# Query tails by transfer, logits summed over heads on GpSimd, guard add on VectorE

## The chip, the cores and the metric

The kernel runs on one core of one Trainium2 chip. The metric is device time in microseconds (us) for one execution, lower is better. Its engines are named by the profile: PE is TensorE (matrix products; PEld its weight loads), DVE is VectorE, ACT is ScalarE, POOL is GpSimd, SP is the engine whose queue issues most DMAs. Each engine takes its instructions strictly in the order in which the program emits them.

## The reference, cut to what matters

```python
# attention: B=4 batches, H=8 heads, S=576 rows, D=64
scores = q @ k.T / 8                       # per batch and head
thresh = scores.max(-1) - tau
scores = where(scores >= thresh, scores, -1e9)
attn = exp(scores - scores.max(-1))
attn = attn / (attn.sum(-1) + 1e-9)        # 1e-9 is the "guard"
x = (attn @ v) laid out as (2304 tokens, 512)

# mixture of 8 experts, two chosen per token
logits = x @ w_gate
noisy = logits + log1p(exp(x @ w_noise)) * noise
top2 = the two largest of the 8; top2_w = softmax of the two (+ 1e-9 in the sum)
x = sum over both of top2_w * (relu(x @ w1[e]) @ w2[e])

# a last two-layer network
h = x @ w_in
out = (max(h, 0) + alpha * min(h, 0)) @ w_out
```

## The kernel before

The first quarter of the kernel, up to about 300 us, is attention with the gating woven into it; after it come the experts and the last network, which are matrix products throughout. The change touches the first quarter alone.

**Units.** Attention is cut into 80 units. A unit is a batch, a pair of heads, and 128 query rows; since 576 is four times 128 plus 64, each batch has a rest of 64 rows, and a "t" unit (16 of the 80) handles the rest of both heads of a pair at once. Units 0 to 15 run over the rows for each head pair in turn; after that the four head pairs of one block of rows follow one another, so that every four units finish one token tile of 128 tokens. There are 18 token tiles; two of them are put together from the rests of two batches (units 16 to 23, and 56 to 63). `tile_of` gives the tile of a unit.

**The hand-written order.** The loop `for i in range(END)` near the end of attention emits unit i's work and, mixed in, that of units before it. On DVE, in iteration i: `d1` (L379, one per head: scaled scores out of PSUM and their extreme), then whatever was put at `(i, -1)`, then `d2` of unit i-1 (L403, one per head: threshold mask times exponential, with the row sum). On PE: transposes of unit i-2 (L421, L423), the scores of unit i+1 (L364), the product with v of unit i-3 (L457, L459), then what was put at `(i, 1)`. On ACT: copies of the transposes (L433, L435), the exponentials of unit i (L390), what was put at `(i, -1)`, the thresholds (L384). `put((j, p), f)` appends f to a list that is run in iteration j at place p: -1 lies between `d1` and `d2`, 0 after the scores of the next unit, 1 at the end. Within one list the order is that of the calls of `put`.

**What follows a finished tile.** When the last head pair of tile T is done in iteration i, `x_stages(T)` gives steps that are put from iteration i+1 on (other offsets for tiles 0 to 4): the guard (L492, POOL, in the iteration before), `turn_rows` (L505, PE transposes), `scale_rows` (L499 reciprocal, L513 multiply by it, then the SP store L515), `logits_mm` (L530), `logits_copy` (L535, ACT), `flip` (L539, a PE transpose that puts tokens on partitions), and `sum_` (L543 and L546, DVE: each of the 8 heads' logits times its inverse sum, then summed over heads).

**Gating.** Tiles are gated in groups (`GROUPS`: three tiles each at first). `gating` puts its steps at a fixed distance from the iteration in which the group's last tile ends (8 for the first group, 4 for most): the exponential and logarithm, `top2` (L597 to L604, DVE), `rank` (PE), `place` (L620, L622 on DVE, L624 on POOL), then `send` (L645), an indirect DMA issued by POOL that scatters the rows of a tile, once for each of the two chosen experts. The rows scattered lie in `xtok_ring`, five slots. The first slot holds zeros at first; so tile 0 has slot 1, tile 4 the slot of the zeros, tile 5 slot 1 again, and so on: `scale_rows` of tile T waits until both scatters of tile T-5 have read the slot. After group four, `close` (L633 to L637, DVE) fixes where later tokens go.

**Splitting and the query tails.** q and k are split into a high and a low part so that products of the reduced-precision type are exact enough: ACT writes the high part (L306, L308), POOL the low part (L316). There are 16 sets (batch and head pair) in eight buffers. `tail_tile` then copies the last 64 query columns of both heads into a block with zeros in the other corners, which the "t" units use: four POOL instructions of 64x64 for each set (L300). Before each split POOL runs `pace` (L712), a one-element copy that waits for the latest `d2`. After the split, SP issues the next load (`next_load`, L282). POOL also copies row sums of the "t" units (L409).

**Late in attention** the first weights of the experts are split in the same way (L171 on ACT, L743 on POOL).

Of the kernel before, what the change touches and what calls it, by code (L numbers as in the profile page):

```python
# [10 lines left out]
OP = mybir.AluOpType  # L11
AX = mybir.AxisListType

B, H, S, D = 4, 8, 576, 64
# [5 lines left out]
NT = N // 128  # L20
# [3 lines left out]
NSET = 8  # L24
SETW = 2688
# [8 lines left out]
def emit(tc, qt, kt, v, tau, wg, wn, noise, w1, w2, w_in, w_out, alpha, out):  # L34
# [3 lines left out]
    pe, dve, act, pool, sp = nc.tensor, nc.vector, nc.scalar, nc.gpsimd, nc.sync  # L38

    def f32(ap):  # L40
        return ap.bitcast(FT)

    with (
# [48 lines left out]
        m_pair = mem.tile([128, 12 * 2048], FR, name="m_pair")  # L92
# [30 lines left out]
        flag = cp.tile([128, 2], FT, name="flag")  # L123
# [128 lines left out]
        lg = cr([NT, 16])  # L252
        wcat, noise_t = cr([HP, 32]), cr([NT, E])
        lt_ring = Ring([cr([128]) for _ in range(3)])
# [39 lines left out]
        def tail_tile(n):  # L294
            t = sets[n]
            t0 = TAIL if (n // HP) % 2 == 0 else 0
            for k in range(2):
                for h in range(2):
                    r = slice(h * 64, h * 64 + 64)
                    pool.tensor_scalar(t[4 + k][r, r], f32(t[k][r, t0:t0 + 64]), 1.0, 1.0, op0=OP.mult, op1=OP.mult)  # L300

        def split_hi(n, part):
            if n not in sets:
# [135 lines left out]
        vps, xts, esum = {}, {}, {}  # L439
# [47 lines left out]
        def x_stages(T):  # L487
            g = {}

            def guard():  # L490
                g["guard"] = True
                pool.tensor_scalar(esum[T], esum[T], 1e-9, 1.0, op0=OP.add, op1=OP.mult)  # L492

            def inverse():
                g["inverse"] = True
                e = esum[T]
                if "guard" not in g:
                    dve.tensor_scalar(e, e, 1e-9, None, op0=OP.add)
                dve.reciprocal(e, e)  # L499

            def turn_rows():
                x = xts[T]
                g["rows"] = psum_t()
                for c in range(HP):
                    pe.transpose(g["rows"][:, c * 128:c * 128 + 128], x[:, c], ident)  # L505

            def scale_rows():
                e = esum[T]
                if "inverse" not in g:
                    inverse()  # L510
                ps = g["rows"]
                xtok[T] = xtok_ring()
                dve.tensor_tensor(xtok[T].rearrange("p (h d) -> p h d", h=H), ps.rearrange("p (h d) -> p h d", h=H),  # L513
                                  e[:, :, None].to_broadcast([128, H, D]), op=OP.mult)
                sp.dma_start(xd[T * 128:T * 128 + 128], xtok[T])  # L515

            def rows():
                turn_rows()
                scale_rows()

            def logits():
                logits_mm()
                logits_copy()

            def logits_mm():
                x = xts[T]
                ps = psum_t()
                g["lp"] = ps
                for c in range(HP):
                    pe.matmul(ps[c * 32:c * 32 + 32, :128], wcat[:, c], x[:, c], start=True, stop=True,  # L530
                              skip_group_check=True)

            def logits_copy():
                g["lt"] = lt_ring()
                act.copy(g["lt"], g["lp"][:, :128])  # L535

            def flip():
                g["ps"] = psum_t()
                pe.transpose(g["ps"][:, :128], g["lt"], ident)  # L539

            def sum_():
                t = lt_ring()
                dve.tensor_tensor(t.rearrange("p (h j) -> p h j", h=H),  # L543
                                  g["ps"][:, :128].rearrange("p (h j) -> p h j", h=H),
                                  esum[T][:, :, None].to_broadcast([128, H, 16]), op=OP.mult)
                dve.tensor_reduce(lg[:, T], t.rearrange("p (h j) -> p j h", h=H), axis=AX.X, op=OP.add)  # L546

            if T < NT - 2:
                return [(-1, 1, guard), (0, 1, turn_rows), (1, -1, scale_rows), (1, 1, logits_mm), (2, -1, logits_copy),
                        (2, 1, flip), (3, -1, sum_)]  # L550
            return [(0, 1, rows), (1, 1, logits), (2, 1, flip), (3, 0, sum_), (0, 0, inverse)]

        def bc8(ap, n):
# [141 lines left out]
        for b in range(1, B):  # L695
            o = 20 * b
# [51 lines left out]
        for n in range(W0):  # L748
            i = 66 + 2 * n
# [36 lines left out]
        for i in range(END):  # L786
            it, iv = i - DT, i - DT - 1
            tiles, outs = 0 <= it < NU, 0 <= iv < NU
            if tiles:
                t_mm(it, 0)  # L790
                a2(it, 0)
            if i < NU:
                for h in range(nh(i)):
                    d1(i, h)
                for h in range(nh(i)):
                    a1(i, h)
            for f, a in at.pop((i, -1), []):
                f(*a)
            if 0 < i <= NU:
                for h in range(nh(i - 1)):  # L800
                    d2(i - 1, h)
            if tiles and nh(it) == 2:
                t_mm(it, 1)
                a2(it, 1)
            if i + 1 < NU:
                s_bank(i + 1)
            if tiles:
                t_mm(it, 2)
            if i < NU:
                thresh(i)  # L810
            if i + 1 < NU:
                s_mm(i + 1)
            if tiles:
                a2(it, 2)
            for f, a in at.pop((i, 0), []):
                f(*a)
            if i == END - 1:
                do_fill()
            if outs:
                pv(iv)  # L820
                if units[iv][2] == HP - 1 or iv < SOLO:
                    T = group_evac(iv)
                    if T is not None:
                        todo = [(i + (1, 3, 5, 7, 2)[T] + d if T < 5 else i + 1 + d, p, f) for d, p, f in x_stages(T)]
                        if T == NT - 1:
                            last_rows.append(todo[0][2])
                            todo = [(i + 1, 0, todo[1][2]), (i + 1, 0, todo[4][2]), (i + 2, 0, todo[2][2]), (i + 2, 0, todo[3][2])]
                        if T == NT - 2:
                            todo = [(i + d, p, f[2]) for (d, p), f in zip(((1, 1), (1, 1), (2, 1), (2, 1)), todo)]
                        for t0, t1 in GROUPS:  # L830
                            if T == t1 - 1:
                                todo += [(i + {3: 8, NT - 1: 3, NT: 2}.get(t1, 4) + d, p, f) for d, p, f in gating(t0, t1)]
                        for j, p, f in todo:
                            put((j, p), f)
            if i >= NU:
                do_fill()
            for f, a in at.pop((i, 1), []):
                f(*a)
# [95 lines left out]
        for n in range(W0, 72):  # L934
            t = 1 + 3 * (n - W0)
# [289 lines left out]
```

## Time and profile before

| | |
|---|---|
| median of 3 runs | 1152.3 us (1151.14 to 1152.39) |
| the profiled execution: its own time | 1154.29 us |
| its span in the profile | 1152.6 us |
| TensorE busy, share of the span | 1125.9 us, 98% |
| VectorE / ScalarE / GpSimd busy | 612.9 / 529.3 / 534.2 us |
| mean granted TensorE clock | 0.997 of full speed |

A timeline row gives the start in us from the span's beginning, the time it took (merged over the count at its end), engine, line, operation, output and inputs, and in brackets the idle time of that engine before it with what released it. A row of the grouped view gives the line, engine, operation, shapes and count, then the busy time in us and the mean of one in ns, then idle time before it by releaser. Busy time of PE holds pipelined matmuls whose ends are modelled; the weight loads show better whether PE stood still.

### The profile page before, as it was taken

Reading aid. Unit: us, or ns where it says so; the run is one execution under the profiler, and the core shown is the slowest. Engines: PE = TensorE matmul, PEld = TensorE weight load, DVE = VectorE, ACT = ScalarE, POOL = GpSimd, SP = SyncE. Lnnn points to the kernel's source line nnn. Section 1 sums busy time; section 2 is a strip of 40 time slices with the busy share of each in tenths; the row PEclk is TensorE's granted clock in tenths of the full one; section 3 lists DMA queues with packets and bytes.
Section 4 is the critical chain, followed back from the end, with each engine's and each line's share of the span. In section 5 each row is a group of like instructions: output and inputs, shape, how many; then the busy total and the mean of one; then the engine's idle time right before and its main releaser. Section 6 shows DMA issues by size and latency. Waiting matters only on the chain. (4 is left out here: it accounts for less than half of the span.)

```text
span 1152.6 us, 20653 instructions
## 1 busy us (share of the span) xinstructions
PE 1125.9 (98%) x7754; PEld 974.4 (85%) x7754; DVE 612.9 (53%) x1316; ACT 529.3 (46%) x1039; POOL 534.2 (46%) x710
## 2 busy tenths in 40 slices
PE   7999999999899999999999999999999999999997
PEld 6887788777798989888989999898888888888886
DVE  6879899688634554354444554444443442442221
ACT  7978888689334444444444444433211111121111
POOL 7556545554625455455555455475332332332221
PEclk9999999999999999999999999999999999999999
DMA  6423222222466766666667575532321221320001
GB/s 211 143 95 117 100 96 84 86 110 97 160 164 186 200 201 189 197 182 196 194 180 202 185 212 170 187 120 69 77 53 51 74 56 45 80 58 20 24 1 39
DMA packets 156553, 141.51 MB, mean 123 GB/s; under 512 B 108576, under 2 KB 109216, under 8 KB 156448
## 3 DMA queue, kind: packets, MB, share of 16 engines
q1 hardware_dynamic: 150400, 120.91, 35.7%
q0 software_dynamic: 5760, 18.88, 4.9%
q8 instruction: 63, 1.03, 0.4%
q14 instruction: 42, 0.34, 0.1%
q10 hardware_dynamic: 288, 0.34, 0.1%
HBM read 97.11 MB, written 42.99 MB: 122 GB/s over the span
## 5 line engine op out<-in xcount | busy, mean ns | idle before, releaser
L214 PE MATMUL ps_t<-m_v,m_pair 128*128 128x384 f32 (+2 forms) x1216 | 220.1, 317 | 0.5 <-DVE m_v L207 0.3
L177 POOL TENSOR_TENSOR m_pair<-m_v,m_pair 128x512 fp32r<-128x512 f32 x104 | 138.8, 1356 | 120.8 <-ACT m_pair L171 100.9
L214 PEld LDWEIGHTS ps_t<-m_v,m_pair 128*128 128x128 f32 x1216 | 186.8, 190 | 8.6 <-ACT m_v L206 0.6
L232 PE MATMUL ps_s<-m_pair,m_hh 128*128 128x512 f32 x528 | 167.5, 390 | 0.0
L1046 DVE TENSOR_SCALAR m_tmp<-ps_t,alpha_t 128x512 f32<-128x512 f32 (+1 forms) x80 | 55.8, 697 | 208.6 <-PE ps_t L214 185.1
L225 DVE SCALAR_TENSOR_TENSOR m_gate<-ps_t,m_hh 128x384 fp32r<-128x384 f32 (+1 forms) x120 | 58.9, 493 | 167.0 <-ACT m_hh L224 166.8
L214 PE MATMUL ps_t<-m_v,m_early 128*128 128x256 f32 (+2 forms) x672 | 127.3, 320 | 0.0
L379 DVE TENSOR_SCALAR_CACHE_REDUCE m_tmp<-ps_s 128x576 f32<-128x576 f32 x144 | 106.1, 755 | 32.0 <-ACT m_last L435 13.2
L403 DVE SCALAR_TENSOR_TENSOR m_hh<-m_tmp,sm,m_hh 128x576 f32<-128x576 f32 x144 | 117.2, 846 | 0.0
L232 PEld LDWEIGHTS ps_s<-m_pair,m_hh 128*128 128x128 f32 x528 | 99.2, 188 | 20.3
L1051 POOL TENSOR_TENSOR m_v<-m_tmp,m_v 128x512 fp32r<-128x512 f32 x39 | 50.5, 1294 | 139.9 <-ACT m_v L1050 139.9
L214 PEld LDWEIGHTS ps_t<-m_v,m_early 128*128 128x128 f32 x672 | 105.8, 189 | 5.1 <-DVE m_v L207 0.4
L390 ACT ACTIVATE m_hh<-m_tmp,sm 128x576 f32<-128x576 f32 x144 | 105.6, 782 | 4.1 <-DVE m_tmp L379 4.1
L1050 ACT CAST m_v<-m_tmp 128x512 fp32r<-128x512 f32 x39 | 24.2, 621 | 173.7 <-DVE m_tmp L1047 173.7
L232 PE MATMUL ps_s<-m_pair,m_gate 128*128 128x512 f32 x264 | 102.9, 390 | 0.0
L364 PE MATMUL ps_s<-m_pair 64*128 64x288 f32 (+1 forms) x864 | 89.5, 319 | 10.2 <-DVE m_tmp L379 5.3
L1051 POOL TENSOR_TENSOR m_gate<-m_tmp,m_gate 128x512 fp32r<-128x512 f32 (+1 forms) x41 | 44.2, 1079 | 115.8 <-ACT m_gate L1050 109.6
L224 ACT ACTIVATE m_hh<-ps_t 128x384 fp32r<-128x384 f32 (+1 forms) x120 | 52.6, 439 | 96.2 <-PE ps_t L214 94.7
L1070 PE MATMUL ps_s<-m_pair,m_v 128*128 128x512 f32 x396 | 95.1, 389 | 0.0
L364 PEld LDWEIGHTS ps_s<-m_pair 64*128 64x128 f32 (+1 forms) x864 | 69.9, 193 | 23.4 <-DVE m_tmp L379 13.9
L1070 PE MATMUL ps_s<-m_pair,m_gate 128*128 128x512 f32 x360 | 88.3, 391 | 0.0
L1070 PEld LDWEIGHTS ps_s<-m_pair,m_v 128*128 128x128 f32 x396 | 74.3, 188 | 15.4
(238 smaller groups left out, 1994.9 us busy)
## 6 DMA issues: line engine op xcount, KB each, us to landing
m_v<-in_w_dram SPq DMA_DIRECT2D x64, 512.0 KB
yg<-m_tmp SPq DMA_DIRECT2D x40, 256.0 KB
m_tmp<-in_w_in_dram SPq DMA_DIRECT2D x16, 512.0 KB
m_tmp<-in_w_out_dram SPq DMA_DIRECT2D x16, 512.0 KB
m_early<-in_kt_dram SPq DMA_DIRECT2D x15, 320.0 KB
yg<-m_gate SPq DMA_DIRECT2D x18, 256.0 KB
m_rows<-xg SPq DMA_DIRECT2D x72, 64.0 KB
out_dram<-m_tmp SPq DMA_DIRECT2D x18, 256.0 KB
```

The costliest lines, as they stand in the source:

```text
L177: eng.tensor_tensor(WL[n][:, w], raw[:, w], f32(WH[n][:, w]), op=OP.subtract)
L214: pe.matmul(ps[:, :n], w[wc[d]][:, col:col + 128], x[xx][:, d, :n], start=(k == 0), stop=(k == 11))
L224: act.activation(h, ps, AF.Relu)
L225: dve.scalar_tensor_tensor(hs[1][:, f * n:f * n + n], ps, 0.0, f32(h), op0=OP.max, op1=OP.subtract)
L232: pe.matmul(ps, a[:, o:o + 128], ww[w][:, c:c + 512], start=(f == 0 and k == 0), stop=(f == nf - 1 and k == 2))
L364: pe.matmul(u["ps", h][:, x, :288], lhs, kk[r, o:o + 288], start=(k == 0), stop=(k == 2))
L379: dve.tensor_scalar(u["sp"][:, h].rearrange("p (a b) -> p a b", a=2), ps[:, :, :288], -0.125, None, op0=OP.mult, op1=OP.min, accum_out=u[" ...
L390: act.activation(u["em"][:, h], u["sp"][:, h], AF.Exp, bias=u["sm"][:, h:h + 1], scale=-1.0)
L403: dve.scalar_tensor_tensor(u["em"][:, h], u["sp"][:, h], sm[:, 2 + h:3 + h], u["em"][:, h], op0=OP.is_le, op1=OP.mult, accum_out=acc)
L1046: dve.tensor_scalar(g, ps, 0.0, alpha_t[:, f:f + 1], op0=OP.min, op1=OP.mult)
L1051: pool.tensor_tensor(h[:, n:2 * n], g, f32(h[:, :n]), op=OP.subtract)
L1070: pe.matmul(ps, h[x][:, t * 128:t * 128 + 128], ww[w][:, c:c + 512], start=(f == 0 and k == 0), stop=(f == 15 and k == 2))
```

## The change

The tails are copied by two SP DMAs for each set (one for each head, both parts at once) in place of four POOL instructions. The guard leaves POOL: VectorE adds it directly ahead of the reciprocal, in a form that also writes an accumulated minimum. `sum_` is replaced for tiles 0 to 15 by an ACT copy out of PSUM (`flip_copy`) and four POOL instructions (`pool_sum`: one multiply of 128x128, then sums of 64, 32 and 16 columns). All groups but the last two are gated one iteration later. Tiles 16 and 17 keep `sum_`.

```diff
         def tail_tile(n):
             t = sets[n]
             t0 = TAIL if (n // HP) % 2 == 0 else 0
-            for k in range(2):
-                for h in range(2):
-                    r = slice(h * 64, h * 64 + 64)
-                    pool.tensor_scalar(t[4 + k][r, r], f32(t[k][r, t0:t0 + 64]), 1.0, 1.0, op0=OP.mult, op1=OP.mult)
+            o = n % NSET * SETW
+            q = m_pair[:, o:o + 2 * S].rearrange("p (k s) -> p k s", k=2)
+            z = m_pair[:, o + SETW - 256:o + SETW].rearrange("p (k s) -> p k s", k=2)
+            for h in range(2):
+                r = slice(h * 64, h * 64 + 64)
+                sp.dma_start(f32(z[r, :, h * 64:h * 64 + 64]), f32(q[r, :, t0:t0 + 64]))
...
         def x_stages(T):
-            def guard():
-                g["guard"] = True
-                pool.tensor_scalar(esum[T], esum[T], 1e-9, 1.0, op0=OP.add, op1=OP.mult)
             def inverse():
                 g["inverse"] = True
                 e = esum[T]
-                if "guard" not in g:
-                    dve.tensor_scalar(e, e, 1e-9, None, op0=OP.add)
+                dve.tensor_scalar(e, e, 1e-9, None, op0=OP.add, op1=OP.min, accum_out=flag[:, 0:1])
                 dve.reciprocal(e, e)
...
+            def flip_copy():
+                g["lt"] = lt_ring()
+                act.copy(g["lt"], g["ps"][:, :128])
+            def pool_sum():
+                t = g["lt"]
+                pool.tensor_tensor(t.rearrange("p (h j) -> p h j", h=H), t.rearrange("p (h j) -> p h j", h=H),
+                                   esum[T][:, :, None].to_broadcast([128, H, 16]), op=OP.mult)
+                pool.tensor_tensor(t[:, 0:64], t[:, 0:64], t[:, 64:128], op=OP.add)
+                pool.tensor_tensor(t[:, 0:32], t[:, 0:32], t[:, 32:64], op=OP.add)
+                pool.tensor_tensor(lg[:, T], t[:, 0:16], t[:, 16:32], op=OP.add)
...
             if T < NT - 2:
-                return [(-1, 1, guard), (0, 1, turn_rows), (1, -1, scale_rows), (1, 1, logits_mm), (2, -1, logits_copy),
-                        (2, 1, flip), (3, -1, sum_)]
+                return [(0, 1, turn_rows), (1, -1, scale_rows), (1, 1, logits_mm), (2, -1, logits_copy),
+                        (2, 1, flip), (3, -1, flip_copy), (3, -1, pool_sum)]
...
-                                todo += [(i + {3: 8, NT - 1: 3, NT: 2}.get(t1, 4) + d, p, f) for d, p, f in gating(t0, t1)]
+                                todo += [(i + {3: 9, NT - 1: 3, NT: 2}.get(t1, 5) + d, p, f) for d, p, f in gating(t0, t1)]
```

## Rows read from the trace of the kernel before

**Rows 1.** The page, part 1: busy us (share of the span) and instructions.
```profile
PE 1125.9 (98%) x7754; PEld 974.4 (85%) x7754; DVE 612.9 (53%) x1316; ACT 529.3 (46%) x1039; POOL 534.2 (46%) x710
```

**Rows 2.** Timeline of PE weight loads over one unit; columns as told above.
```profile
175.29 0.83 PEld L364 LDWEIGHTS ps_s<-m_pair 64*128 64x128 f32 x12 [0.17 <-DVE es L499]
176.28 0.85 PEld L457 LDWEIGHTS ps_v<-m_last,m_v 128*64 128x64 f32 x16 [0.16 <-issue]
...
177.88 0.86 PEld L421 LDWEIGHTS ps_t<-ident,m_hh 128*128 128x128 f32 x8 [0.20 <-ACT m_gate L584]
...
179.01 0.82 PEld L364 LDWEIGHTS ps_s<-m_pair 64*128 64x128 f32 x12 [0.17 <-issue]
```

**Rows 3.** Grouped view by form, DVE, 0 to 300 us.
```profile
L513 DVE TENSOR_TENSOR m_gate<-ps_t,es 128x512 f32<-128x512 f32 x17 | 11.8, 692 | 3.9 <-DMA xg<-m_gate,posi 2.3
L546 DVE TENSOR_REDUCE m_rows<-m_rows 128x16 f32<-128x128 f32 x17 | 6.4, 376 | 0.6
L543 DVE TENSOR_TENSOR m_rows<-ps_t,es 128x128 f32<-128x128 f32 x17 | 4.9, 286 | 0.5 <-PE ps_t L539 0.5
L499 DVE RECIPROCAL es<-es 128x8 f32<-128x8 f32 x17 | 3.4, 197 | 2.5 <-POOL es L492 2.5
L379 DVE DVE_READ_ACCUMULATOR m_tmp<-ps_s 128x1 f32 x144 | 11.9, 83 | 0.0
L637 DVE TENSOR_SCALAR m_gate<-m_gate 1x8 bf16<-1x8 f32 x1 | 1.2, 1200 | 0.0
L498 DVE TENSOR_SCALAR es<-es 128x8 f32<-128x8 f32 x1 | 0.6, 566 | 0.0
```

**Rows 4.** The same view, POOL, 0 to 300 us.
```profile
L300 POOL TENSOR_SCALAR m_pair<-m_pair 64x64 fp32r<-64x64 f32 x64 | 24.6, 384 | 5.5 <-DMA xg<-m_gate,posi 2.3
L492 POOL TENSOR_SCALAR es<-es 128x8 f32<-128x8 f32 x16 | 5.8, 361 | 1.2
L592 POOL TENSOR_TENSOR m_gate<-m_gate,m_rows 128x24 f32<-128x24 f32 x5 | 2.0, 406 | 0.4
L590 POOL TENSOR_TENSOR m_gate<-m_gate 128x24 f32<-128x24 f32 x5 | 1.2, 233 | 0.2
```

**Rows 5.** The same view, ACT, 0 to 300 us.
```profile
L535 ACT COPY m_rows<-ps_t 128x128 f32<-128x128 f32 x17 | 4.3, 254 | 0.3 <-PE ps_t L530 0.3
```

**Rows 6.** One line's instructions (ns, min/median/max), L403.
```profile
L403 DVE SCALAR_TENSOR_TENSOR m_hh<-m_tmp,sm,m_hh x144: 805/815/1557, 11.1 to 294.4; 128x576 f32<-128x576 f32 x144
```

**Rows 7.** Timeline of POOL, 109 to 117.5 us.
```profile
112.21 1.34 POOL L645 DMA_INDIRECT xg<-m_gate,posi  x1 [0.20 <-issue]
...
113.88 0.18 POOL L712 COPY m_gate<-es 1x1 f32<-1x1 f32 x1
...
116.43 0.97 POOL L645 DMA_INDIRECT xg<-m_gate,posi  x1 [0.21 <-issue]
```

**Rows 8.** Timeline of DVE, 110 to 119 us.
```profile
117.02 0.69 DVE L513 TENSOR_TENSOR m_gate<-ps_t,es 128x512 f32<-128x512 f32 x1 [2.35 <-DMA xg<-m_gate,posi]
```

**Rows 9.** Timeline of POOL, 213 to 222.5 us.
```profile
214.21 1.25 POOL L645 DMA_INDIRECT xg<-m_gate,posi  x1 [0.16 <-POOL m_gate L644]
...
217.25 0.18 POOL L409 COPY es<-sm 64x1 f32<-64x1 f32 x1 [1.57 <-DMA xg<-m_gate,posi]
```

**Rows 10.** Timeline of DVE, 215 to 222.5 us.
```profile
218.78 0.20 DVE L499 RECIPROCAL es<-es 128x8 f32<-128x8 f32 x1 [2.51 <-POOL es L492]
```

**Rows 11.** Timeline of PE, 216.4 to 225 us.
```profile
216.46 1.04 PE L364 MATMUL ps_s<-m_pair 128*128 128x288 f32 x6
...
221.05 0.90 PE L421 MATMUL ps_t<-ident,m_hh 128*128 128x128 f32 x4 [2.32 <-DVE m_hh L403]
...
221.82 1.79 PE L364 MATMUL ps_s<-m_pair 128*128 128x288 f32 x6
```

**Rows 12.** Windows: us, busy (x instructions) of each engine, PEclk, DMA share, GB/s.
```profile
220.00:240.00 20.00, 18.45 (x228) 15.29 (x229) 16.15 (x53) 12.51 (x30) 8.20 (x28) 0.91 0.28 106
```

**Rows 13.** Timeline of DVE, 185 to 191 us.
```profile
185.71 0.29 DVE L597 MAX8 mx<-m_gate 128x8 f32<-128x8 f32 x3
...
186.79 0.81 DVE L403 SCALAR_TENSOR_TENSOR m_hh<-m_tmp,sm,m_hh 128x576 f32<-128x576 f32 x1
```

**Rows 14.** Timeline of PE, 188 to 191 us.
```profile
189.88 0.66 PE L421 MATMUL ps_t<-ident,m_hh 128*128 128x128 f32 x4 [0.58 <-DVE m_gate L620]
```

## The prediction, made before the change was run

> **What bounds the kernel now.** I began with the page's busy shares: TensorE is busy for 98% of the span [rows 1]. Such a share says little about one stage, so next I read the weight loads through one attention unit, because a matmul's end is modelled and a load's start is not. From one unit's score loads to the next unit's, 175.29 to 179.01, 3.72 us, no gap in the rows shown is above 0.20 us, though VectorE, ScalarE and "issue" take turns as the releaser [rows 2]. So an ordinary attention unit is TensorE-bound; VectorE and ScalarE come close but have slack. Third, I looked through the waits for places where TensorE really stands still in the first 300 us, since only there can this change gain or lose. Three belong to it: a wait of VectorE at 117 us for a scatter [rows 8], one at 218 us for the guard on GpSimd [rows 10], and a short one, twice alike, where transposes wait for `place` [rows 14]. After 300 us nothing is touched, and what attention loses or gains is taken as passing through to the end.
>
> **The tails.** 64 GpSimd instructions go, 24.6 us busy [rows 4]. GpSimd is not the bound (46%, rows 1) and nothing in the waits was released by a tail copy, so their removal by itself is worth nothing; I take 0. The 32 new DMAs sit in SP's order ahead of the next load, each waiting for the low split. The loads run several splits ahead and the "t" units use a tail units later, so also 0. The price if that cover fails: a unit, 3.72 us [rows 2].
>
> **The sum over heads.** VectorE loses L543 and L546, 286 + 376 ns, for 16 tiles: 10.6 us busy [rows 3]. If all of it lay on the path, that would be the gain; if TensorE covers all, nothing. In an ordinary unit TensorE covers it; in the one-head units of tiles 0 to 3 and 12 a little may show. I take -0.4. ScalarE gains 16 copies like L535, 254 ns, 4.1 us busy [rows 5], in the place where the logits copy already stands one unit earlier: 0, at most +4.1. GpSimd gains 64 instructions: by the nearest rows, 233 ns (L590) to 406 ns (L592) each [rows 4], so 0.9 to 1.6 us a tile; I take 1.3, the multiply being the longest.
>
> **The guard.** VectorE gains 16 small instructions plus their accumulator reads. The nearest rows are the reciprocal on the same 128x8 (197 ns) with the read (83 ns), 0.28 us; the upper end is L498, the same add without accumulation, 566 + 83 ns [rows 3]. I take 0.28, 4.5 us busy, hidden beneath TensorE in ordinary units (+10.4 at worst, if all showed at the upper end).
>
> Rows first, for the contention of the two engines: L403 has median 815 ns and maximum 1557 [rows 6], L498 took 566 and L637, eight elements on one partition, 1200 [rows 3]. Something holds VectorE for whole instructions. The Trainium skill (page "SBUF — State Buffer", section "Who interferes with whom") says GpSimd shares a port pair with VectorE; a plain `tensor_scalar` can enter a two-port mode and be blocked, the accumulating form cannot, and a VectorE instruction with two SBUF inputs contends with a GpSimd instruction that reads SBUF. By it the guard costs the lower price, which is also the nearest row; it speaks against `pool_sum`, which is a rival below.
>
> **What goes at 218 us.** The reciprocal waits 2.51 us for GpSimd's guard [rows 10], because GpSimd is held in front of it: a copy of row sums waits 1.57 us for a scatter to land [rows 9]. TensorE stands still for 2.32 us [rows 11], and then runs slowly: the score group takes 1.79 us where the one before took 1.04 [rows 11], and the granted clock of that window is 0.91 [rows 12], so part of it ran at 1.2 GHz instead of 2.4. The slow stretch costs between 0.75 (1.79 - 1.04) and 1.8 us (0.09 x 20); I take 1.2. With the guard on VectorE both go: -3.5. What is late next is GpSimd itself: its last scatter of the group moves one unit later, the row-sum copy waits for that one, and the last split of batch 3 stands behind it. I give back 1.3 for it, an estimate between 0 (nothing waits) and 3.5 (all of it). Sum: -2.2.
>
> **What is added at 117 us.** The slot of tile 5 is that of tile 0, so its L513 waits until tile 0's second scatter has landed: issued at 112.21 + 1.34 = 113.55, L513 starts at 117.02, 3.5 us later, after 2.35 us of VectorE idle [rows 7, 8]. The first group's gating now starts at distance 9, so these scatters move one unit on, to about where tile 1's pair stands, whose second ends at 116.43 + 0.97 = 117.40 [rows 7]. Ahead of them GpSimd now also does the 1.3 us of tile 4's `pool_sum`; against this, the earlier scatters no longer hold L712 until 113.88 [rows 7]. These roughly cancel, with 0.2 over: 117.6. From issue end to release it is 3.5 us here and 1.8 at 215.46 to 217.25 [rows 9]; both happen, so I take the middle, 2.7. L513 then starts at 120.3 instead of 117.0: +3.3 (from +2.4 with 1.8 to +4.1 with 3.5). TensorE now stands still for longer than the 2.32 us that were followed by the slow clock, so I add the same 1.2 (0 to 1.8). Sum: +4.5.
>
> **`top2` moves onto the units that scale.** For groups two and three, `top2` takes 186.79 - 185.71 = 1.08 us [rows 13] and stands now in a unit without scaling, and `place` in the next one, in front of the scaling; transposes wait 0.58 us for it [rows 14]. After, `top2` stands in the scaling unit. Between the end of that unit's second L379 and L620 VectorE then does 1.08 + 0.28 + 0.2 + 0.7 + two L403 (about 1.5 with pipelining) + two L379 (about 1.4) + 0.2 = 5.3 us. TensorE comes back to the transposes after about a unit, 3.8. The wait grows from 0.6 to 1.5: +0.9, two times, +1.8 (0 if there is slack ahead of that L379, +3 with an L403 held).
>
> **`close`** moves one unit on, behind tile 13's scaling; its L637 alone took 1.2 us [rows 3]. Between 0 and +1.2, I take +0.4.
>
> **Sum.** 0 - 0.4 + 0 + 0 - 2.2 + 4.5 + 1.8 + 0.4 = +4.1. In the profiled execution's own terms 1154.3 + 4.1 = 1158.4; that execution lies 2.0 above the median of the runs, so against the median I say 1156.4.
>
> **Rivals.** (1) The guard's wait decides, and the kernel gets faster. The split behind the row-sum copy is early enough, so that all 3.5 us come back; GpSimd, rid of four tail copies in the units before 110 us, sends tile 0's rows as soon as `place` is done, and L513 is only 1 us later, with no slow clock; the two `top2` moves find slack. With the -0.4 of the sums: -3.5 + 1.0 - 0.4 = -2.9, so 1149.4. For it: each tail copy takes 0.38 us [rows 4] and they stand directly ahead of those scatters. Against it: `place` comes a whole unit later whatever GpSimd does. It decides from where the scatter's landing is less than 3.5 us later than now. (2) It stays the same: the two waits cancel (+3.3 and -3.5) and the rest is covered: about 1152. For it: the bound of ordinary units is TensorE, whose work is unchanged [rows 2]. Against it: both added terms end in a TensorE wait that the trace already shows. (3) `pool_sum` collides: 64 GpSimd instructions that nothing paces hold L403 as it has been held, 1557 - 815 = 0.74 us [rows 6], once for each tile. Where VectorE has been freed of 0.66 this cancels; if both L403 of a unit are held, 16 x (2 x 0.74 - 0.66) = 13 us on VectorE, of which I let a third through TensorE's cover: +4.4, 1160.8. The rule of the Trainium skill above is what would do it. Against it: most L403 run beside some GpSimd work and the median stays 815. (4) The tail DMAs come late behind a store on SP that waits: 1160.1 (one unit); little speaks for it.
>
> **How the numbers follow.** The forecast has 0.46, rival 1 0.16, rival 2 0.25, rivals 3 and 4 together 0.13. About 0.2% (2.3 us) is what a measurement of this kernel can tell from no change. Faster by more: rival 1, 0.16. Same: 0.25. Slower: 0.46 + 0.13 = 0.59. The forecast's own range is the landing (+2.4 to +4.1), the clock (0 to 1.8), the return at 218 us (-3.5 to 0) and the `top2` units (0 to 3), most of it within +1 to +8. The range that leaves 2 in 10 out goes a little into rival 1 and to rival 3: 1150.3 to 1161.5.
>
> **What would show it.** Right: the wait in front of tile 5's L513 is 5 to 6 us instead of 2.35, and its window has a clock below 1.00; the reciprocal near 218 us waits for nothing; L620 is the releaser of two PE waits near 1.5 us; ordinary units still take 3.4 to 3.7 us. Wrong: L513 of tile 5 starts at about its old time; or L403's median rises above 815 ns and the loads' gaps in ordinary units grow (rival 3); or units at other places stop for a DMA from `m_pair` (rival 4). It would be most wrong if ordinary units got shorter, since then VectorE and not TensorE was their bound.

## The result, and the profile after

The changed kernel is slower: 1163.37 us median of five runs (1162.13 to 1165.84), beside 1151.30 (1150.44 to 1152.39) for the kernel before in the same comparison, ratio 1.0106, 95% interval 1.0094 to 1.0118, so +12.1 us. The direction was forecast, the size was not: 1156.4 was said, and the range ended at 1161.5.

The profiled execution took 1162.43 us, span 1160.7, only 8.1 above the profiled execution of before. That one had lain 3.0 above the median of this comparison, this one lies 0.9 below its own; together that is the 12.1. I set the two traces against each other by the start of every unit's first scaling pass (L379 before, L381 after, counted from unit 0). The difference is 0.0 us at unit 32, +6.0 at 36, +6.4 at 48, +7.9 at 60, +5.1 at 61, +7.0 at 66, +9.4 at 76, +8.5 at 79 and +8.2 at the end. So everything happens in a few places of attention, and in this execution the expert stage passes it on nearly unchanged.

The page of the kernel after, part 1, answers to [rows 1]:

```profile
PE 1128.5 (97%) x7754; PEld 976.1 (84%) x7754; DVE 608.7 (52%) x1318; ACT 531.5 (46%) x1055; POOL 528.3 (46%) x694
```

No busy sum moved by more than 6 us. The time lies in idle stretches and in the clock, so the waits have to be read. VectorE's timeline, at the places of [rows 8, 10] and at two more:

```profile
121.41 0.69 DVE L510 TENSOR_TENSOR m_gate<-ps_t,es 128x512 f32<-128x512 f32 x1 [6.36 <-DMA xg<-m_gate,posi]
...
150.66 0.29 DVE L606 MAX8 mx<-m_gate 128x8 f32<-128x8 f32 x3
...
152.23 0.69 DVE L510 TENSOR_TENSOR m_gate<-ps_t,es 128x512 f32<-128x512 f32 x1
...
224.19 0.20 DVE L496 RECIPROCAL es<-es 128x8 f32<-128x8 f32 x1
...
271.15 3.02 DVE L405 SCALAR_TENSOR_TENSOR m_hh<-m_tmp,sm,m_hh 128x576 f32<-128x576 f32 x1
```

Tile 5's scaling (L510, L513 before) now waits 6.36 us for its slot, where it waited 2.35. At 150.66 `top2` stands directly ahead of the guard, reciprocal and scaling of one tile. The reciprocal at 224.19 waits for nothing. At 271.15 a mask pass (L405, L403 before) of usually 0.81 us took 3.02. TensorE's timeline, three waits behind these places, and one row of undisturbed transposes for comparison:

```profile
122.98 1.93 PE L423 MATMUL ps_t<-ident,m_hh 128*128 128x128 f32 x8 [5.08 <-DVE m_hh L405]
...
149.98 1.04 PE L423 MATMUL ps_t<-ident,m_hh 128*128 128x128 f32 x8
...
155.93 0.66 PE L423 MATMUL ps_t<-ident,m_hh 128*128 128x128 f32 x4 [1.42 <-DVE m_gate L629]
...
234.11 1.07 PE L366 MATMUL ps_s<-m_pair 64*128 64x288 f32 x12 [1.64 <-DVE m_tmp L381]
```

Eight transposes after the first wait took 1.93 us; eight take 1.04 at 149.98. That is the clock, as the windows show (columns as in [rows 12]):

```profile
100.00:120.00 20.00, 17.38 (x220) 14.01 (x216) 13.14 (x50) 15.08 (x35) 10.55 (x26) 1.00 0.49 141
120.00:140.00 20.00, 17.02 (x186) 14.55 (x186) 16.86 (x46) 13.47 (x31) 11.57 (x24) 0.91 0.32 116
...
220.00:240.00 20.00, 18.24 (x231) 15.05 (x225) 12.74 (x44) 12.78 (x36) 13.58 (x39) 0.91 0.25 94
```

A window at 0.91 has one stretch at 1.2 GHz and costs 0.09 x 20 = 1.8 us. Before there was one such window, 220 to 240, behind the guard's wait; now there is one behind tile 5's wait, and the one at 220 to 240 is there again though the guard's wait is gone. ScalarE's and GpSimd's timelines say why:

```profile
231.14 0.22 ACT L593 ACTIVATE m_gate<-m_gate 128x24 f32<-128x24 f32 x1 [2.17 <-POOL m_gate L586]
```

```profile
113.17 0.40 POOL L544 TENSOR_TENSOR m_rows<-m_rows,es 128x128 f32<-128x128 f32 x1 [1.45 <-ACT m_rows L540]
...
114.69 0.86 POOL L318 TENSOR_TENSOR m_pair<-m_early,m_pair 128x320 fp32r<-128x320 f32 x1
...
115.76 1.21 POOL L654 DMA_INDIRECT xg<-m_gate,posi  x1 [0.18 <-issue]
...
117.27 0.97 POOL L654 DMA_INDIRECT xg<-m_gate,posi  x1 [0.21 <-issue]
...
230.89 0.21 POOL L586 TENSOR_SCALAR m_gate<-m_gate 128x24 f32<-128x24 f32 x1
...
269.71 1.06 POOL L654 DMA_INDIRECT xg<-m_gate,posi  x1 [5.22 <-DVE m_hh L405]
...
270.92 1.28 POOL L752 TENSOR_TENSOR m_early<-m_v,m_early 128x512 fp32r<-128x512 f32 x1
...
272.29 1.26 POOL L752 TENSOR_TENSOR m_early<-m_v,m_early 128x512 fp32r<-128x512 f32 x1
```

The logarithm of group four (L593) stands in ScalarE's queue 2.17 us for GpSimd's L586; VectorE and TensorE run dry behind it, 1.64 us at 234.11. Tile 0's sends [rows 7: second one at 112.21] now begin behind the wait for `flip_copy`, `pool_sum` and a split, and the second ends at 118.24. And the 3.02 us of the mask pass lie over two weight splits of GpSimd, 270.92 to 273.55, which come back to back behind group four's last send; GpSimd stood 5.22 us in front of that send. The grouped views give the new instructions (by form, 0 to 310 us):

```profile
L496 DVE RECIPROCAL es<-es 128x8 f32<-128x8 f32 x17 | 3.4, 203 | 0.6
L495 DVE TENSOR_SCALAR_CACHE_REDUCE es<-es 128x8 f32<-128x8 f32 x17 | 2.6, 154 | 0.0
```

```profile
L544 POOL TENSOR_TENSOR m_rows<-m_rows,es 128x128 f32<-128x128 f32 x16 | 7.3, 457 | 29.1 <-ACT m_rows L540 29.1
L546 POOL TENSOR_TENSOR m_rows<-m_rows 128x64 f32<-128x64 f32 x16 | 5.1, 321 | 1.3
L547 POOL TENSOR_TENSOR m_rows<-m_rows 128x32 f32<-128x32 f32 x16 | 4.0, 252 | 1.3
L548 POOL TENSOR_TENSOR m_rows<-m_rows 128x16 f32<-128x16 f32 x16 | 3.9, 247 | 1.3
```

`pool_sum` takes 457 + 321 + 252 + 247 ns, 1.28 us a tile (1.3 was said). What was not priced is the last column of its first row: GpSimd stands 29.1 us in all in front of it, waiting for ScalarE's copy, with everything that is queued behind.

### The profile page after: what moved, and what is told of

It reads as the page before. It is cut to its first block, busy times and chain, and to the rows that moved or that the text cites. A ratio compares the mean times of both kernels' runs of the same rounds, so it can differ in the third digit from the quotient of the medians.

```text
span 1160.7 us, 20692 instructions
## 1 busy us (share of the span) xinstructions
PE 1128.5 (97%) x7754; PEld 976.1 (84%) x7754; DVE 608.7 (52%) x1318; ACT 531.5 (46%) x1055; POOL 528.3 (46%) x694
## 5 line engine op out<-in xcount | busy, mean ns | idle before, releaser
L381 DVE TENSOR_SCALAR_CACHE_REDUCE m_tmp<-ps_s 128x576 f32<-128x576 f32 x144 | 106.3, 754 | 40.2 <-ACT m_last L437 9.8
L405 DVE SCALAR_TENSOR_TENSOR m_hh<-m_tmp,sm,m_hh 128x576 f32<-128x576 f32 x144 | 121.3, 875 | 0.0
L423 PE MATMUL ps_t<-ident,m_hh 128*128 128x128 f32 x576 | 81.9, 283 | 9.0 <-DVE m_hh L405 5.8
```

The source lines that it names most:

```text
L381: dve.tensor_scalar(u["sp"][:, h].rearrange("p (a b) -> p a b", a=2), ps[:, :, :288], -0.125, None, op0=OP.mult, op1=OP.min, accum_out=u[" ...
L405: dve.scalar_tensor_tensor(u["em"][:, h], u["sp"][:, h], sm[:, 2 + h:3 + h], u["em"][:, h], op0=OP.is_le, op1=OP.mult, accum_out=acc)
L423: pe.transpose(ps[:, j * 128:j * 128 + 128], emf[:, o + j * 128:o + j * 128 + 128], ident)
```

## The experiments

My theory was that the later gating carries the loss, by tile 5's slot and a stretch at the lower clock behind it. The rivals were GpSimd's new work beside VectorE and the tail transfers on SP. "Over" and "under" are differences of medians against the kernel before in the same comparison.

| run | what it is | us against before | ratio (95% interval) |
|---|---|---|---|
| | the change | +12.1 | 1.0106 (1.0094 to 1.0118) |
| e_dist | distances alone | +12.0 | 1.0111 (1.0095 to 1.0126) |
| e_sum | sum over heads alone | +5.4 | 1.0043 (1.0029 to 1.0056) |
| e_guard | guard alone | +2.2 | 1.0022 (1.0013 to 1.0031) |
| e_tails | tails alone | +1.5 | 1.0017 (1.0008 to 1.0026) |
| e_nodist | change without distances | +3.6 | 1.0032 (1.0019 to 1.0044) |
| y_tgd | change without sum | +10.3 | 1.0088 (1.0074 to 1.0102) |
| y_gsd | change without tails | +17.8 | 1.0148 (1.0131 to 1.0164) |
| y_tsd | change without guard | +15.6 | 1.0140 (1.0125 to 1.0156) |
| x_ring6 | change, six slots | +6.7 | 1.0057 (1.0043 to 1.0071) |
| e_rest4 | change, distances 9 and 4 | +3.9 | 1.0037 (1.0023 to 1.0051) |
| z_six4 | change, six slots, 9 and 4 | -0.3 | 1.0000 (0.9991 to 1.0009) |
| z_six | before, six slots | -1.3 | 0.9988 (0.9979 to 0.9997) |
| z_sixg | before, six slots, guard | -1.3 | 0.9987 (0.9978 to 0.9996) |
| x_c1 | z_sixg, later logarithm | -3.1 | 0.9979 (0.9969 to 0.9989) |
| x_c2 | x_c1 with tails | -0.9 | 0.9997 (0.9988 to 1.0006) |

### One part alone

**Distances** (e_dist):

```diff
-  {3: 8, NT - 1: 3, NT: 2}.get(t1, 4) + d
+  {3: 9, NT - 1: 3, NT: 2}.get(t1, 5) + d
```

> The kernel before with the gating distances 9 and 5 alone. Theory (later gating): the sends of tile 0 end near 118 us instead of 113, tile 5's scaling waits some 6 us for its ring slot, TensorE stands still for some 5 us and is granted the lower clock after it; this run then carries most of the loss, 1158 to 1163 us, and its unit-by-unit shift has the step of some 4.5 us at unit 33. Rival (GpSimd's new work): the distances alone move nothing on the path, 1151 to 1153 us, no step at unit 33. Rival (tails late): the same, 1151 to 1153 us.

+12.0: as much as the whole change, a little above what was expected. VectorE's timeline:

```profile
118.28 0.69 DVE L513 TENSOR_TENSOR m_gate<-ps_t,es 128x512 f32<-128x512 f32 x1 [4.15 <-DMA xg<-m_gate,posi]
...
223.08 0.20 DVE L499 RECIPROCAL es<-es 128x8 f32<-128x8 f32 x1 [3.69 <-POOL es L492]
...
266.74 0.20 DVE L499 RECIPROCAL es<-es 128x8 f32<-128x8 f32 x1 [2.66 <-POOL es L492]
```

The step is +1.3 at unit 33 and +2.5 at unit 36, not 4.5 and 6.0: without `pool_sum` in front of them the sends are earlier, and tile 5 waits 4.15 us. The rest comes later. GpSimd's guard is caught behind a send twice, 3.69 and 2.66 us (2.51 once before, rows 10). The second of these sends is the last of group four, and the profile names what it waited for:

```profile
260.17 0.84 SPq L193 DMA_DIRECT2D m_v<-xg  x2
```

```profile
265.43 1.00 POOL L645 DMA_INDIRECT xg<-m_gate,posi  x1 [5.69 <-DMA m_v<-xg]
```

`x_load` (L193), put at iteration 70, reads the first expert's rows out of `xg`. With distance 4 the last send of group four, which writes `xg`, is put at iteration 69, ahead of it; with distance 5 it is put at 70, behind it, and waits until the read has landed. Every run with the later distance has this wait, 5.2 to 5.7 us (also where the profile names VectorE as the releaser), and no run with distance 4 has it. Here the shift grows by 3.3 us at unit 73. So the later gating carries the loss, but not by tile 5's slot alone.

**Sum over heads** (e_sum):

```diff
-  (3, -1, sum_)]
+  (3, -1, flip_copy), (3, -1, pool_sum)]
```

> The kernel before with only the sum over heads on GpSimd from a ScalarE copy, distances 8 and 4 as before. Theory (later gating): no change within 2 us, 1150 to 1153 us, unless GpSimd's queue, which stands until the copy is done, makes the sends late by itself: then the step at unit 33 is here too, with 1155 to 1158 us. Rival (GpSimd's work beside VectorE costs each time): 11 to 15 tiles at 0.7 us, 1159 to 1162 us, spread evenly over the units.

+5.4, in the branch I had called the exception, and by another queue than I named. ScalarE's timeline, one row of several:

```profile
220.86 0.22 ACT L584 ACTIVATE m_gate<-m_rows 128x24 f32<-128x24 f32 x1 [3.10 <-POOL m_rows L551]
```

At distance 4 the group's exponential stands in ScalarE's queue until `pool_sum` has ended (four waits, 8.0 us). With distance 5, in the changed kernel, the same wait is 0.4 us in all. The rival has a trace too: the mask passes above 0.95 us have 7.6 us of excess over 0.82, where it was 4.0 before; but the shift does not grow evenly over the units, so most of it does not reach TensorE.

**Guard** (e_guard):

```diff
-  (-1, 1, guard), (0, 1, turn_rows), ...
+  (0, 1, turn_rows), ...
-  if "guard" not in g:
-      dve.tensor_scalar(e, e, 1e-9, None, op0=OP.add)
+  dve.tensor_scalar(e, e, 1e-9, None, op0=OP.add, op1=OP.min, accum_out=flag[:, 0:1])
```

> The kernel before with only the guard add moved from GpSimd to VectorE, in the accumulating form. Every theory has the wait of 3.5 us near 218 us gone and with it the stretch at the lower clock that follows it: 1147 to 1149.5 us. If the next late thing stands right behind it, 1151 us.

Missed: 2.2 over, where 3 to 5 under was expected. Unit 61 is 2.7 us earlier, as said. But then, on ScalarE and on TensorE:

```profile
223.97 0.23 ACT L579 ACTIVATE m_gate<-m_gate 128x24 f32<-128x24 f32 x1 [3.09 <-POOL m_gate L572]
```

```profile
225.81 0.47 PE L534 MATMUL ps_t<-ident,m_rows 128*128 128x128 f32 x1 [2.10 <-ACT m_rows L530]
```

The logarithm waits for the same late GpSimd queue, and 2.3 of the 2.7 us are gone one unit later. Another 2.3 us were lost at units 42 and 43, where ScalarE stood for 4.2 us instead of 1.8; see the last section.

**Tails** (e_tails):

```diff
-  pool.tensor_scalar(t[4 + k][r, r], f32(t[k][r, t0:t0 + 64]), 1.0, 1.0, ...)   # x4
+  sp.dma_start(f32(z[r, :, h * 64:h * 64 + 64]), f32(q[r, :, t0:t0 + 64]))      # x2
```

> The kernel before with only the query tails copied by transfers from SP. Theory (later gating): nothing, 1150.5 to 1152.5 us. Rival (the tail transfers come late behind a store on SP's queue): 1155 to 1160 us, with waits of TensorE at the tail units 16 to 19, 36 to 43 and so on.

+1.5, between the two. Not the tails come late but the loads behind them. SP's timeline, first one row of the kernel before, then this run's; VectorE's timeline, and a window:

```profile
105.13 0.33 SPq L282 DMA_DIRECT2D m_early<-in_qt_dram  x1
```

```profile
106.43 1.25 SPq L302 DMA_DIRECT2D m_pair<-m_pair  x2
107.72 0.59 SPq L282 DMA_DIRECT2D m_early<-in_qt_dram  x1
...
110.78 0.60 SPq L282 DMA_DIRECT2D m_early<-in_kt_dram  x1
```

```profile
119.23 0.69 DVE L515 TENSOR_TENSOR m_gate<-ps_t,es 128x512 f32<-128x512 f32 x1 [4.85 <-DMA xg<-m_gate,posi]
```

```profile
116.00:118.00 2.00, 1.15 (x20) 0.91 (x18) 0.00 (x0) 1.21 (x4) 0.30 (x1) 1.00 1.00 397
```

SP holds at the tail transfers until the low split is done, so the load that was issued at 105.13 before is issued at 107.72. The loads then fill the DMA engines (share 1.00, where it was 0.36 before) while tile 0's rows are being scattered. Though the second send was issued at 111.32, 0.9 us earlier than before, tile 5 waits 4.85 us instead of 2.35. In the two profiles that costs 2.9 us at unit 60, of which 2.8 come back by unit 63: the reciprocal there waits 1.25 us instead of 2.51, and no stretch at the lower clock follows.

### One part left out

Each is the change with one hunk of its diff taken back (e_nodist: the distances; y_tgd: `flip_copy` and `pool_sum`; y_gsd: `tail_tile`; y_tsd: the guard).

```diff
-  .get(t1, 5) + d            # e_nodist: {3: 8, ...}.get(t1, 4)
-  pool_sum                   # y_tgd: sum_
-  sp.dma_start (tails)       # y_gsd: pool.tensor_scalar x4
-  dve guard                  # y_tsd: pool guard
```

> The changed kernel with both distances as before, 8 and 4: tails, sum over heads and guard alone. Theory (the later gating carries the loss): 3 to 7 us over before, of which the sum over heads, for which ScalarE's exponentials now wait, is 5, the tails 1.5, and the guard gives back up to 3. Rival (tails, sum and guard carry it together): 10 us or more over before.

> The changed kernel without the sum over heads on GpSimd (it is on VectorE as before): tails, guard and distances 9 and 5. Theory (later gating first, GpSimd's sum second): the sends of tile 0 no longer wait behind the sum, tile 5's wait shrinks by some 1 to 2 us, and the score passes that GpSimd's reads stretch (1.5 to 3.0 us instead of 0.8, 4.5 us more in all than before) are short again near 263 to 280 us: 7 to 10 us over before. Rival (the distances carry all of it): 11 to 12.5 us over before.

> The changed kernel with the tails copied on GpSimd as before: guard, sum over heads and distances 9 and 5. Theory (the tail transfers hold SP's queue, so 1.7 MB of loads start 2.6 us later and run over the scatters of tile 0): tile 5's wait of 6.4 us shrinks by 1 to 3 us, 8 to 11 us over before. Rival (GpSimd gets the tail copies back, four of 0.42 us for each head pair, and everything behind them is later): 11 to 14 us over before.

> The changed kernel with the guard on GpSimd as before: tails, sum over heads and distances 9 and 5. Theory (the guard's wait grows with the distance, as where the distances stand alone: 3.7 us near 223 us and 2.7 us near 267 us): both waits stand there, each in TensorE's time and one with a stretch at the lower clock, 15 to 19 us over before. Rival (the guard is hidden here): 11 to 12.5 us over before, like the changed kernel.

Without the distances 8.5 of the 12.1 are gone, as expected. Without the sum 1.8 are gone (expected 2 to 5; the rival's bound of 11 us isn't reached either); the two runs' intervals overlap, so 1.8 is barely clear of noise. In its profile 3.8 us are gone by unit 79 and 2.7 are lost again behind it, where the window 300 to 320 has a granted clock of 0.91. Without the guard 3.5 us come on top, as expected; VectorE's timeline of that run has both waits:

```profile
225.14 0.20 DVE L501 RECIPROCAL es<-es 128x8 f32<-128x8 f32 x1 [2.74 <-POOL es L494]
...
270.73 0.20 DVE L501 RECIPROCAL es<-es 128x8 f32<-128x8 f32 x1 [4.14 <-POOL es L494]
```

Without the tails it is 5.7 us worse, beyond the rival's range too; my theory had them as a cost, and this falls. With the tail copies and `pool_sum` both on GpSimd, its splits get late as well, and TensorE waits for one, which elsewhere happens only once, for 0.3 us in x_ring6:

```profile
236.01 1.57 PE L364 MATMUL ps_s<-m_pair 128*128 128x288 f32 x5 [1.72 <-POOL m_pair L316]
```

So the tails by transfer cost 1.5 us alone and are worth 5.7 beside the three other parts. That they do it by making room on GpSimd for `pool_sum` fits this row; tails and `pool_sum` as a pair were not run.

### The two repairs

Six slots (x_ring6), and the distance of the first group alone (e_rest4); z_six4 has both:

```diff
-  xtok_ring = Ring([cg([DM]) for _ in range(5)])
+  xtok_ring = Ring([cg([DM]) for _ in range(6)])
-  gate_tmp = Ring([cg([240]) for _ in range(2)])
+  gate_tmp = Ring([cl([240]), cg([240])])
...
-  {3: 9, NT - 1: 3, NT: 2}.get(t1, 5) + d
+  {3: 9, NT - 1: 3, NT: 2}.get(t1, 4) + d
```

> The changed kernel with a sixth slot in the ring of scaled rows, so that tile 5's scaling doesn't wait for the sends of tile 0 (one of the two gating scratch tiles moves to m_last for it). Theory (the later sends reach tile 5's slot): its wait of 6.4 us near 121 us goes, with TensorE's stand-still of 5 us and the 3.4 us at the lower clock after it; some 6 us of the 12 over before go, 5 to 7 us over before are left. Rival (GpSimd's queue and the scratch traffic carry the loss, the wait only absorbs slack): within 1.5 us of the changed kernel, 10.5 to 13 us over before.

> The changed kernel with the distance 9 for the first group as changed and 4 for the groups after it, as before. Theory (the first group's distance makes tile 5's wait, the others' only move top2): the step at unit 33 and its stretch at the lower clock stay, the two pauses of 1.4 us at units 41 and 53 shrink to 0.6, but ScalarE now waits 2 to 3 us for the sum over heads in the groups at 4: 8 to 13 us over before. Rival (the later groups' distance carries the loss): 3 to 6 us over before.

> The changed kernel with six slots and the distances 9 and 4: both repairs together. Theory (two separate costs that add: tile 5's slot is worth 5 of the 12, the later groups' distance 7 to 8): the two gains add, 2 us under to 1 us over before. Rival (they are one cost, seen twice): 3 to 4 us over before, as with the better repair alone.

Six slots take 5.4 of the 12.1 us: tile 5's scaling waits for no send. That step is shown. e_rest4 went against the theory: +3.9, in the rival's range, though tile 5's wait is there:

```profile
119.97 0.69 DVE L510 TENSOR_TENSOR m_gate<-ps_t,es 128x512 f32<-128x512 f32 x1 [5.28 <-DMA xg<-m_gate,posi]
```

```profile
149.52 0.66 PE L423 MATMUL ps_t<-ident,m_hh 128*128 128x128 f32 x4 [0.56 <-DVE m_gate L629]
```

The `top2` pauses are 0.56 instead of 1.42 us as expected; the exponential's waits came back, 1.92 us at most, and cost less than they did in e_sum; ScalarE no longer waits at the logarithm, and after a TensorE pause of 1.51 us at 224 us no second stretch at the lower clock follows. The later groups' distance carries 8.2 us, tile 5's slot 5.4. z_six4 shows that these are two costs and not one: together the repairs give 12.4 (13.6 if they added in full), the change then costs nothing, -0.3 us, and no gain is left of it either.

### Versions of the kernel before

Each adds to the one before it. z_six: six slots, as above. z_sixg: with the guard of the change. x_c1: with the logarithm of group four, and the GpSimd step `noisy` behind it, one unit later. x_c2: with the tails too.

```diff
-  plan = [(d, 1, f) for d, f in enumerate(first[:4])] + ...
+  plan = [(d, 1, f) for d, f in zip((0, 1, 3, 4) if t1 == FIRST else range(4), first)] + ...
```

> The kernel before with six slots alone. Theory (a wait of tile 5 is paid in full): its 2.35 us wait goes, TensorE's 1.5 us at units 32 and 33 with it: 1 to 2 us under before. Rival (the next thing stands there, or the guard near 218 us takes it back): within 0.5 us of before.

> The kernel before with six slots and the guard on VectorE, without the later logarithm. Theory (the guard's wait only hides ScalarE's wait for the same GpSimd queue near 222 us): no better than with six slots alone, 0.5 to 2.5 us under before. Rival (the later logarithm is worth nothing): 3 us under before, as with it.

> The kernel before with six slots in the ring of scaled rows, the guard on VectorE, and the logarithm of the fourth group one unit later, so that ScalarE does not wait 3 us behind GpSimd near 222 us. Theory (each stand-still named so far is paid in full, with the stretch at the lower clock behind it): 3 to 5 us under before. Rival (behind each wait that goes stands another): within 1 us of before.

> The kernel with six slots, guard on VectorE and the later logarithm, and the tails by transfers as well, sum over heads and distances as before. Theory (the tails cost only through tile 5's slot, which six slots set free): 2.5 to 4.5 us under before, no worse than without the tails. Rival (the later loads hold TensorE or another wait): 0 to 2 us under before.

Six slots alone give 1.3 us. The guard on top gives nothing more, and x_c1, whose only difference to that is the later logarithm with `noisy`, gives 3.1. Those two were not timed in one comparison, so the 1.8 us between them is a difference of two differences, and their intervals overlap (0.9969 to 0.9989 and 0.9978 to 0.9996): it is not clear of noise. The rows of the three, VectorE of z_six, then ScalarE of z_sixg and of x_c1:

```profile
217.15 0.20 DVE L499 RECIPROCAL es<-es 128x8 f32<-128x8 f32 x1 [2.48 <-POOL es L492]
```

```profile
219.75 0.22 ACT L579 ACTIVATE m_gate<-m_gate 128x24 f32<-128x24 f32 x1 [3.08 <-POOL m_gate L572]
```

```profile
220.13 0.22 ACT L579 ACTIVATE m_gate<-m_gate 128x24 f32<-128x24 f32 x1 [0.19 <-POOL m_gate L572]
```

One late GpSimd queue is waited for by two engines, 2 us apart. The rows show that the wait of one hides the other's: in z_sixg unit 61 starts 2.7 us earlier against z_six and 2.3 of it are lost at unit 62, in x_c1 they are kept. That the medians gain when both are gone is likely, and not shown beyond noise. x_c1, 1148.85 us (1148.36 to 1151.09, beside 1151.98 for the kernel before), beats both kernels. x_c2 missed: the tails cost 2.2 us there, and not through the slot; against x_c1's profile it loses 2.3 us at units 42 and 43 (the last section) and 1.1 at unit 68.

## Why the prediction went wrong

In the profiled executions' terms the forecast was +4.1 and the result +8.1; the median missed by 7.0. The direction and the mechanism at tile 5 were right. What failed: tile 5's term was too small, too little was given back for the late GpSimd queue at 218 us, a wait of group four's last send had no term at all, and 2.0 us were taken off on the way to the median. By the steps:

- **Bound and method: right.** Ordinary units are TensorE's and stayed so. The 10.6 us of VectorE work that went gave nothing, and the signs named in advance are there: a wait of 6.36 at tile 5 (5 to 6 said, a little more came), a clock under 1.00 behind it, no wait of the reciprocal, and two `place` waits of 1.4 (1.5 said).
- **Tile 5: right mechanism, +6.0 instead of +4.5.** Its L510 starts 4.4 us later, not 3.3. The second send ends at 118.24 (117.6 said): `pool_sum` does not only run ahead of the sends, GpSimd first waits 1.45 us for the copy. From there to L510 it is 3.2 us (2.7 said). The stretch at 1.2 GHz cost 1.8 by the window, not 1.2. Six slots returned 5.4.
- **`top2`: +1.8 from unit 36 to 60, as said.** Right.
- **The guard: the step that failed in attention.** "What is late next is GpSimd itself" was right, and 1.3 was given back for it. But I did not look for who else waits for that queue: the logarithm on ScalarE, which stood 2.73 us there in the trace of before at the same time:

```profile
221.01 0.22 ACT L584 ACTIVATE m_gate<-m_gate 128x24 f32<-128x24 f32 x1 [2.73 <-POOL m_gate L577]
```

Of the 2.7 us won at unit 61, 1.8 were lost by unit 66, and the stretch at the lower clock that I had struck out came back behind the new pause. Net -0.9, said -2.2.

- **Units 66 to the end: +1.2, `close` was given +0.4.** `close` cost more than that, and it doesn't show in the sum. TensorE's and VectorE's timelines, before and then after:

```profile
241.49 1.05 PE L364 MATMUL ps_s<-m_pair 64*128 64x288 f32 x12 [1.17 <-DVE m_tmp L379]
245.82 1.06 PE L364 MATMUL ps_s<-m_pair 64*128 64x288 f32 x12 [0.29 <-DVE m_tmp L379]
```

```profile
243.23 1.20 DVE L637 TENSOR_SCALAR m_gate<-m_gate 1x8 bf16<-1x8 f32 x1
```

```profile
255.82 0.30 PE L425 MATMUL ps_s<-ident,m_hh 128*128 128x128 f32 x1 [1.09 <-DVE m_tmp L381]
256.41 1.06 PE L366 MATMUL ps_s<-m_pair 64*128 64x288 f32 x12 [0.29 <-DVE m_tmp L381]
```

```profile
253.74 1.26 DVE L646 TENSOR_SCALAR m_gate<-m_gate 1x8 bf16<-1x8 f32 x1
```

Behind `close` TensorE waits 0.29 us before and 1.09 + 0.29 after. The wait of 1.17 us before lies ahead of `close` and is absent after, so the shift is +7.0 at unit 66 and +6.8 at unit 70. What is left comes later, where mask passes are stretched by GpSimd's weight splits: 1.94, 3.02 and 1.97 us at units 71, 73 and 75. This is rival 3 with another partner, the 128x512 splits. At units 71 and 75 a split starts right behind `pool_sum` and into a mask pass; at unit 73, the longest, two splits stand behind group four's last send and its wait of 5.22 us, for which the prediction had no term. Without `pool_sum` (y_tgd) the pass at unit 73 still takes 2.26 us, and those at 71 and 75 are short again. On VectorE the excess over 0.82 us, of passes above 0.95, is 8.5 us in all (4.0 before). The Trainium skill ("SBUF — State Buffer", "Who interferes with whom") states that a VectorE instruction with two SBUF inputs contends with a GpSimd instruction that reads SBUF, and these rows agree. How little of it reaches the end it doesn't say.

- **Tails at 0, sum at -0.4: wrong, each with both signs.** Alone they cost 1.5 and 5.4. I asked whether their engines were late, not whose queue stands behind them: SP's loads behind the tails, ScalarE's exponential behind the sum. That the later distances shorten this last wait (8.0 us in e_sum, 0.4 in the change) was not seen.
- **From the profile to the median: 2.9 of the 7.0.** I took 2.0 off because the profiled execution of before lay that much above its median. But part of that excess was a stretch at the lower clock which only some of its runs have: in 21 later runs those with a granted clock of 0.999 took 1151.6 to 1153.0 us, those with 0.997 took 1153.2 to 1154.2. The rest isn't traced; the kernel's own median lay between 1151.3 and 1153.6 us from one comparison to the next. The changed kernel has more pauses that can be followed by one: its five runs go from 0.996 (1162.1) to 0.993 (1165.8), and its profiled one is among the best. So here the added pauses add to the median what the one profile doesn't show.

That the two repairs together return the whole loss (z_six4) is shown. How the 8.2 us of the later groups' distance divide among `top2`, the logarithm, `close`, the last send, the weight splits and the clock is read from the traces' steps and was not measured one by one; no run has the last send alone put back.

## What to carry to other kernels

When a step is moved in a hand-ordered program, go through every engine's queue and ask what stands behind the moved instruction and who waits for that; here each of the four edits was paid for, or lost its gain, on another queue than the one it was meant to relieve. A moved write to a shared buffer can also fall behind a read that it used to precede, as group four's last send did. Before counting a removed wait as gain, look for the next engine that waits for the same late producer at that time. This kernel, 98% TensorE, pays for a pause twice, once as idle time and, in some runs, once more as a stretch at 1.2 GHz; so compare medians with their granted clocks, not two profiles.

## What was not expected of the hardware

- **GpSimd beside VectorE.** A mask pass with two SBUF inputs of 128x576 takes 0.81 us, 1.94 where one GpSimd subtraction of 128x512 lies over it, 3.02 with two (units 71 and 73 of the change).
- **The landing of a scatter.** From the end of the second send's issue to tile 5's scaling it was 3.5 us before [rows 7, 8], 2.0 with the distances alone (116.32 to 118.28), 3.2 in the change (118.24 to 121.41), and 6.8 with the tails alone (112.46 to 119.23), where the loads filled the DMA engines.
- **The lower clock after a pause is not certain.** TensorE pauses of 1.50 and 1.64 us in x_ring6's profile were followed by none; its five runs go from 1155.35 us at 0.999 to 1159.02 at 0.995.
- **Open:** in e_guard and x_c2 ScalarE stands at unit 41 for 4.1 to 4.2 us where it stands 1.8 in the kernel before and 1.7 in x_c1, and 2.3 us are lost. Counted from unit 41, the sends around it lie the same to 0.03 us in x_c1 and x_c2, so they are hardly the cause. TensorE's weight loads stand there too, 0.36 and 0.25 us in e_guard, 0.55 and 0.23 in x_c2, each put down to "issue", at a granted clock of 1.00; in x_c1 no gap there is above 0.17. What holds them is not known. It is much of why the guard alone is slower, and of what the tails cost in x_c2.
